# Row maxima of windowed scores: four heads' blocks of 32 queries against one head's blocks of 128

## The chip, the cores and the metric

The kernel runs on one core of a Trainium2 chip. The metric is the device time of one execution in microseconds (us), the median of several runs. The core has five engines that run side by side, each with its own queue of instructions in fixed order: TensorE (PE in the profile; PEld is its weight load), VectorE (DVE), ScalarE (ACT), GpSimd (POOL) and SyncE (SP), which here only issues DMAs. Matmul results go to PSUM, from which VectorE and ScalarE read.

## What is computed

Two independent parts stand side by side in the output. Part A is attention with 32 heads of 18 dimensions over 2048 positions, in a sliding window of 256 keys; part B is a state-space convolution over 2048 positions in 576 channels, done as a product in the frequency domain.

```python
H = 32; Dh = D // H; W = 256                 # S = 2048, D = 576
scores = jnp.einsum("bhqd,bhkd->bhqk", q, k) * (Dh ** -0.5)
mask = (idx[:, None] - idx[None, :] >= 0) & (idx[:, None] - idx[None, :] < W)
scores = jnp.where(mask[None, None], scores, -1e9)
p = _softmax(scores, axis=-1)
o = jnp.einsum("bhqk,bhkd->bhqd", p, v)
...
return jnp.concatenate([a, b], axis=-1)
```

The softmax needs the largest score of each query among its 256 keys (or something near it). The change is in how that maximum is found.

## The kernel before

Up to about 475 us the kernel projects x to q, k and v (in split halves of 16 bits), builds the convolution's tables and transforms u and the convolution's taps. The attention follows, with the convolution's frequency products and inverse transform woven in.

The attention has 16 units, `i` from 0 to 15: `hf, g = divmod(i, 8)`, half of the positions (1024 queries) and a group of four heads. A unit's tensor `Q` is 128 x 2 x 1024: heads lie in two row halves `u` (rows 0 to 53 and 64 to 117, three parts of 18 dimensions in each) and two column planes `b`. `K` has the same layout with 1280 columns, 256 of them ahead of the unit's first query. Row 54 of each half of `Q` holds the row maximum, row 54 of `K` a large negative constant, so that the score matmuls of `scores` (L738) subtract the maximum by themselves. Three sets of `Q` and `K` rotate.

`gmax(i)` computes the maxima of unit `i`. It begins by copying `Q` into `qb`, block-diagonally (L688): for each 32 queries of a plane, 64 columns, the first 32 with the upper half's head and the last 32 with the lower half's. Then it goes over 32 blocks `t` of 32 queries. For each block one PSUM tile of the pool `ring` (three buffers of 128 x 512) takes two matmuls, one for each plane, of up to 288 keys (L697), so that its 128 rows are four heads by 32 queries. VectorE adds a bias that masks the triangles at both ends and takes the maximum over the 288 in one instruction, whose sum register is then read out (L704). After every two blocks the generator yields. At the end the 128 x 32 maxima are scaled, transposed in 32 x 32 blocks (L711, L712), and four DMAs on SP's queue, due with the next item, write them into row 54 of `Q` (L715; in the profile they appear under L133, which issues what is due).

`attention` (L835) writes out the order by hand. It goes over 96 items, six for each unit (two halves `c` of 512 queries, three banks of score blocks) and merges in each item several generators in proportion: `scores` of item n (TensorE, then the exponentials on ScalarE, L740, then masks on GpSimd, L749), `gmax` of the unit after next, `values` of item n-2 (L761), and a share of `conv`. `gmax(i + 2)` starts in item 3 of unit i and ends by item 3 of unit i+1, with 17 yields over six items; `gmax(0)` runs before the items, merged with the rest of the taps' transform `s1k` (L520), and `gmax(1)` in the first three items. `load_unit(i + 2)` (L676, L677) issues the loads of a unit in item 0 of unit i. The normalisation `norm` of a finished unit (L797 on, with L812, L820 and L823 on VectorE) advances one step per item.

`conv` shares `ring` with `gmax`: two matmul tiles of the signal (L561) that ScalarE copies out (L588), two of the taps (L561 again) that VectorE multiplies with them from PSUM (L591 to L594), sums on GpSimd (L598, L599), and two tiles of the inverse transform (L569) that ScalarE copies out (L571). The output projection (L967) uses `ring` too. A tile of `ring` is handed out in the order of the program, and a matmul into it waits until the tile three places earlier has been read.

Of the kernel before, what the change touches and what calls it, by code (L numbers as in the profile page):

```python
# [11 lines left out]
F32 = mybir.dt.float32  # L12
F16 = mybir.dt.float16
BF = mybir.dt.bfloat16
I32 = mybir.dt.int32
AF = mybir.ActivationFunctionType
OP = mybir.AluOpType
AX = mybir.AxisListType
# [21 lines left out]
def constants():  # L40
    c = {}
    tau = 2 * np.pi
    l1, l2, f1, f2 = np.arange(32), np.arange(64), np.arange(32), np.arange(64)
    ph = -tau * np.outer(l1, f1 + 0.25) / 32
    w1 = np.zeros((128, 2, 128))
    for s in range(4):
        w1[s * 32:s * 32 + 32, 0, s::4] = np.cos(ph)
        w1[s * 32:s * 32 + 32, 1, s::4] = np.sin(ph)
    w2 = np.zeros((128, 32, 128))
    i1 = np.zeros((128, 32, 128))  # L50
    for f in range(32):
        ph = -tau * np.outer(l2, f + 0.25 + 32 * f2) / 2048
        co, si = np.cos(ph), np.sin(ph)
        w2[0:64, f, 0:64], w2[64:128, f, 0:64] = co, -si
        w2[0:64, f, 64:128], w2[64:128, f, 64:128] = si, co
        i1[0:64, f, 0:64], i1[64:128, f, 0:64] = co.T, si.T
        i1[0:64, f, 64:128], i1[64:128, f, 64:128] = -si.T, co.T
    ph = tau * np.outer(f1 + 0.25, l1) / 32
    i2 = np.zeros((128, 64))
    for p in range(2):  # L60
        i2[p * 64:p * 64 + 32, p * 32:p * 32 + 32] = np.cos(ph) / 2048
        i2[p * 64 + 32:p * 64 + 64, p * 32:p * 32 + 32] = -np.sin(ph) / 2048
    mult = {"c_cm": np.arange(64), "c_ct": np.arange(32) + 0.5, "c_ca": np.r_[64 * np.arange(8), 512 * np.arange(4)],
            "c_cp": np.r_[np.zeros(8), np.full(4, 31.5)]}
    for nm, v in mult.items():
        t = np.zeros((3, GC, GC, len(v)))
        for g in range(GC):
            t[:, g, g] = v
        c[nm] = t.reshape(96, GC, len(v))
    bias = np.zeros((128, 2, 32))  # L70
    for p in range(128):
        bias[p, 0, :p % 32 + 1] = -1e30
        bias[p, 1, p % 32 + 1:] = -1e30
    c["c_w1"], c["c_w2"], c["c_i1"], c["c_i2"] = w1, w2, i1, i2
    c["c_id"], c["c_bias"] = np.eye(128), bias
    return {k: np.ascontiguousarray(v.astype(ml_dtypes.bfloat16 if k in mult else np.float32)) for k, v in c.items()}
# [40 lines left out]
class Kernel:  # L117
# [527 lines left out]
    def att_setup(self):  # L645
        nc, a, ap = self.nc, self.a, self.p["att"]
        self.ident = ap.tile([128, 128], F32, name="ident")
        nc.sync.dma_start(self.ident, a["c_id"])
        self.bias = ap.tile([128, 288], F32, name="bias")
        nc.vector.memset(self.bias, 0.0)  # L650
        for e in range(2):
            nc.sync.dma_start(self.bias[:, 256 * e:256 * e + 32], a["c_bias"][:, e])
        self.qb = ap.tile([128, 2, 32, 64], F16, name="qb")
        nc.gpsimd.memset(self.qb, 0.0)
        self.sets = []
        for b in range(3):
            d = {"Q": ap.tile([128, 2, HQ], F16, name="Q%d" % b), "K": ap.tile([128, 2, HK], F16, name="K%d" % b)}
            nc.vector.memset(d["Q"], 0.0)
            for h in (32, 96):
                nc.vector.memset(d["K"][h:h + 32].bitcast(I32), 0xF800F800 - (1 << 32))  # L660
            self.sets.append(d)
        self.od = self.p["dram"].tile([2, D, L], F16, name="od")
# [19 lines left out]

    def gmax(self, i):

        nc, (hf, g), d = self.nc, divmod(i, 8), self.sets[i % 3]
        m = self.p["m"].tile([128, 32], F32, name="m")
        for u in range(2):
            nc.vector.tensor_copy(self.qb[64 * u:64 * u + 54, :, :, 32 * u:32 * u + 32],  # L688
                                  d["Q"][64 * u:64 * u + 54].rearrange("p b (t q) -> p b t q", q=32))
        yield  # L690
        pair = []
        for t in range(32):
            ps = self.p["ring"].tile([128, 512], F32, name="r")
            k0 = 32 * t if hf > 0 or t >= 8 else 256
            n = 32 * t + 288 - k0
            for b in range(2):
                nc.tensor.matmul(ps[64 * b:64 * b + 64, :n], self.qb[:, b, t, :], d["K"][:, b, k0:k0 + n],  # L697
                                 start=True, stop=True, skip_group_check=True)
            pair.append((t, n, ps))
            if t % 2 == 0:  # L700
                continue
            for t, n, ps in pair:
                jk = self.p["m"].tile([128, 288], F32, name="jk")
                nc.vector.tensor_tensor_reduce(out=jk[:, :n], in0=ps[:, :n], in1=self.bias[:, 288 - n:], scale=1.0,  # L704
                                               scalar=-3e38, op0=OP.add, op1=OP.max, accum_out=m[:, t:t + 1])
            pair = []
            yield
        yield
        m16 = self.p["m"].tile([128, 32], F16, name="m16")
        mt = self.p["m"].tile([128, 32], F16, name="mt")  # L710
        nc.vector.tensor_scalar(m16, m, 2.0 ** -15, None, op0=OP.mult)  # L711
        nc.vector.transpose(mt, m16)  # L712
        for j in range(4):
            r = 64 * (j % 2) + 54
            self.after(1, nc.sync.dma_start, d["Q"][r:r + 1, j // 2].rearrange("o (s q) -> o s q", q=32),  # L715
                       mt[32 * j:32 * j + 32])
        yield

    BL = [(0, 0, 0, 1), (128, 2, 0, 3), (512, 1, 0, 2), (768, 4, 2, 4), (1024, 3, 1, 4), (1408, 5, 3, 4)]
# [379 lines left out]
```

## Time and profile before

| what | us |
|---|---|
| three runs | 1017.26, 1021.78, 1023.51 (median 1021.78) |
| the profiled execution | 1019.01 |
| its span in the profile | 1017.3 |
| mean granted TensorE clock in it | 0.972 of full |

The profile shows one execution. For each engine it gives the time in which it worked and, before each instruction, the idle time and what ended it. The chain of waits follows the work back from the last instruction to what released each step. A matmul of two or four pieces is recorded as several matmuls, and a few per cent of the records are missing. Busy times include the overlap of neighbours on one engine only once.

### The profile page before, as it was taken

The page shows a single profiled execution, that of the slowest core. Times are in us where ns is not written, and L with a number is a line of the kernel's source. Part 1 is how long each engine was busy: PE and PEld are TensorE (multiplying, and loading weights), DVE is VectorE, ACT ScalarE, POOL GpSimd, SP SyncE. Part 2 cuts the span into 40 slices and gives each one's busy share as a digit, 9 for nine tenths or more (in the row PEclk, how much of TensorE's full clock was granted, in tenths as well). Part 3 has the DMA queues.
Part 4 walks back from the last instruction along what each step waited for, and adds up shares of the span by engine and source line. Part 5 has one row for each costly group of instructions (what it writes and reads, how often), then busy time and mean ns, then how long its engine had stood idle before and what let it go on. Part 6 is the DMA issues. An engine that isn't in the chain of part 4 may idle for free.

```text
span 1017.3 us, 26963 instructions
## 1 busy us (share of the span) xinstructions
PE 836.2 (82%) x10364; PEld 447.1 (44%) x10364; DVE 691.9 (68%) x1821; ACT 561.8 (55%) x901; POOL 590.6 (58%) x727
## 2 busy tenths in 40 slices
PE   0287979888899999788888888778888999988687
PEld 0034645464566557454433333323333444444245
DVE  5689487567574566557677778767777766668454
ACT  1456656557666765235555555555555655634470
POOL 2119557475686677101657675748676757676680
PEclk9999989999999999799999999989999999999899
DMA  8824535424443542746465675645555584578863
GB/s 299 254 69 122 141 91 131 98 74 121 123 105 76 133 100 74 226 169 199 122 152 126 177 172 144 164 119 150 136 136 152 132 189 114 157 199 231 229 181 126
DMA packets 139240, 150.35 MB, mean 148 GB/s; under 512 B 37464, under 2 KB 106248, under 8 KB 138344
## 3 DMA queue, kind: packets, MB, share of 16 engines
q1 hardware_dynamic: 131144, 131.75, 48.3%
q0 software_dynamic: 6512, 15.04, 5.6%
q10 hardware_dynamic: 1456, 1.84, 0.6%
q8 instruction: 82, 1.34, 0.6%
q14 instruction: 46, 0.38, 0.1%
HBM read 86.30 MB, written 61.01 MB: 145 GB/s over the span
## 4 chain that ended last, share of the span: by engine, by line
PE 27%; DVE 11%; DMA 6%; issue 6%; ACT 3%; SPq 2%; POOL 2%; DVEq 0%; ACTq 0%; POOLq 0%
PE r L697 5%; PE po L761 5%; PE r L967 5%; PE r L561 3%; PE r L569 3%; PE ST L738 3%; DVE jk L704 2%; PE pp L520 2%; DVE qb L688 2%; ACT P L740 1%; DVE osb L820 1%; DMA out_dram<-t 1%; DVE t L591 1%; DMA raw<-in_wo_dram 1%; DMA tx<-gx 1%
## 5 line engine op out<-in xcount | busy, mean ns | idle before, releaser
L704 DVE CUSTOM_DVE_ANT_0 jk<-r,bias 128x288 f32<-128x288 f32 (+7 forms) x512 | 200.1, 434 | 90.4 <-PE r L697 88.3
L749 POOL TENSOR_SCALAR_AFFINE_SELECT P<-P 128x512 f32<-128x512 f32 x240 | 167.8, 728 | 149.3 <-ACT P L740 146.6
L740 ACT ACTIVATE P<-ST,esc 128x1024 f32<-128x1024 f32 (+1 forms) x192 | 202.7, 1060 | 91.8 <-PE ST L738 91.2
L441 POOL TENSOR_TENSOR m<-A,tr 128x1024 f32<-128x1024 f32 x72 | 144.3, 2026 | 84.1 <-PE kp L479 84.0
L697 PE MATMUL r<-K,qb 128*64 128x288 f16 (+7 forms) x1024 | 129.1, 295 | 45.2 <-DVE qb L688 12.0
L697 PEld LDWEIGHTS <-qb 128*64 128x64 f16 x1024 | 59.8, 109 | 128.4 <-issue 69.4
L761 PE MATMUL po<-P,V 128*32 128x256 f32 (+2 forms) x1408 | 99.9, 397 | 16.3 <-ACT osb L769 7.0
L598 POOL TENSOR_TENSOR Y<-t,t 64x288 f32<-64x288 f32 x64 | 55.0, 859 | 77.9 <-DVE t L593 76.0
L479 PE MATMUL kp<-Q,m 128*32 128x64 f32 x4608 | 80.3, 221 | 10.9 <-issue 2.8
L479 PEld LDWEIGHTS kp<-Q,m 128*32 128x32 f32 x4608 | 69.3, 110 | 41.7 <-issue 22.4
L738 PE MATMUL ST<-Q,K 64*128 64x384 f16 (+2 forms) x704 | 72.7, 280 | 0.0
L382 DVE TENSOR_TENSOR k<-x,k 128x512 f32<-128x512 f32 (+1 forms) x54 | 34.1, 642 | 36.7 <-ACT k L381 36.3
L144 ACT ACTIVATE g<-pp 128x288 f32<-128x288 f32 x96 | 37.9, 414 | 37.4 <-PE pp L520 29.9
L761 PEld LDWEIGHTS po<-P,V 128*32 128x32 f32 x1408 | 36.3, 110 | 50.3 <-issue 34.2
L419 POOL TENSOR_TENSOR tr<-tr,mab 128x768 f32<-128x768 f32 x18 | 33.4, 1858 | 42.5 <-ACT tr L388 42.5
L179 PE MATMUL pp<-xh,wh 128*128 128x512 f16 x180 | 48.4, 387 | 9.4 <-ACT xh L210 8.9
L599 POOL TENSOR_TENSOR Y<-t,t 64x288 f32<-64x288 f32 x64 | 53.3, 832 | 3.7
L179 PEld LDWEIGHTS <-wh 128*128 128x128 f16 x324 | 31.5, 99 | 51.2 <-issue 17.8
L383 DVE TENSOR_SCALAR ab<-k 128x512 int32<-128x512 int32 (+1 forms) x54 | 50.5, 947 | 0.4
L561 PE MATMUL r<-tx,w 128*64 128x288 f32 x256 | 42.4, 441 | 9.0 <-ACT X L588 4.8
L520 PE MATMUL pp<-ut,w 128*128 128x288 f32 x128 | 40.4, 437 | 10.0 <-DVE qst L341 6.9
L821 ACT ACTIVATE oh<-osb 128x512 f16<-128x512 f32 x26 | 16.4, 632 | 55.9 <-DVE osb L820 55.3
(169 smaller groups left out, 1729.1 us busy)
## 6 DMA issues: line engine op xcount, KB each, us to landing
qd<-qst SPq DMA_DIRECT2D x72, 128.0 KB
gx<-g SPq DMA_DIRECT2D x32, 288.0 KB
gk<-g SPq DMA_DIRECT2D x32, 288.0 KB
tx<-gx SPq DMA_DIRECT2D x32, 288.0 KB
tk<-gk SPq DMA_DIRECT2D x32, 288.0 KB
h<-ho SPq DMA_DIRECT2D x16, 576.0 KB
Q<-qd SPq DMA_DIRECT2D x32, 216.0 KB
raw<-in_x_dram SPq DMA_DIRECT2D x16, 320.0 KB
```

The lines of the kernel that those rows point to most:

```text
L179: self.nc.tensor.matmul(ps, u, v, start=(i == 0), stop=(i == len(ops) - 1))
L441: self.nc.gpsimd.tensor_tensor(m, A[:, ch, a0:a0 + 8].unsqueeze(3).to_broadcast(sh), tr[:, ch, part, 0:8].unsqueeze(2).to_broadcast(sh), o ...
L479: nc.tensor.matmul(kp[32 * st:32 * st + 32, c % 2 * JJ2 + j, :], m[:, ch, a0:a0 + 32], Q[:, ch, term % 2, :], start=(term == 0), stop=(ter ...
L520: nc.tensor.matmul(ps, self.w1[:, part, :], src[:, o:o + k], start=True, stop=True)
L561: nc.tensor.matmul(ps[64 * par:64 * par + 64], w2[:, par, 64 * part:64 * part + 64], t[:, par, 2 * hs:2 * hs + 2, :], start=True, stop=True)
L598: nc.gpsimd.tensor_tensor(Y[par][0:64], t1[sl, 0], t2[sl, 0], op=OP.subtract)
L697: nc.tensor.matmul(ps[64 * b:64 * b + 64, :n], self.qb[:, b, t, :], d["K"][:, b, k0:k0 + n], start=True, stop=True, skip_group_check=True)
L704: nc.vector.tensor_tensor_reduce(out=jk[:, :n], in0=ps[:, :n], in1=self.bias[:, 288 - n:], scale=1.0, scalar=-3e38, op0=OP.add, op1=OP.max ...
L738: nc.tensor.matmul(ps[:, u, o:o + n], d["K"][h, jp, k0:k0 + 128], d["Q"][h, jp, q0:q0 + n], start=True, stop=True, skip_group_check=True)
L740: nc.scalar.activation(pt[:, 2 * jp:2 * jp + 2, lo:hi], ps[:, :, lo:hi], AF.Exp, scale=self.esc)
L749: nc.gpsimd.affine_select(v, v, pattern=[[0, 4], [sg, 128]], compare_op=OP.is_ge, fill=0.0, base=-1 if far else 0, channel_multiplier=-sg)
L761: nc.tensor.matmul(self.po[32 * j:32 * j + 32, t0 * 128:t1 * 128], V[:, kb * 76 + 19 * j:kb * 76 + 19 * j + 32], pt[:, j, o:o + (t1 - t0) ...
```

## The change

The maxima are computed one head at a time, for 128 queries in a tile. `qb`, its memset and its copies are gone; the matmuls take 128 columns of `Q` (54 rows of one half) as weights and up to 384 keys of the same half of `K`, and a step makes two PSUM tiles, one for each row half. There are again 16 steps and yields per unit, with two tiles each. In a full tile the first 128 columns are the far keys and the last 128 the near ones; query p may see far key j if j > p and near key j if j <= p. So the two triangles fit together: where the mask constant is not zero (near keys that are not allowed), a predicated copy writes the far key's score over the near one's in PSUM, and one maximum over columns 128 to 383 follows. Tiles at the very beginning of the sequence, with 128 or 256 keys, are done as before with a bias of the new shape. The maxima come out in another arrangement, so eight DMAs of 16 pieces each write them into `Q`, instead of four of 32.

```diff
-    bias = np.zeros((128, 2, 32))
+    bias = np.zeros((128, 256))
     for p in range(128):
-        bias[p, 0, :p % 32 + 1] = -1e30
-        bias[p, 1, p % 32 + 1:] = -1e30
+        bias[p, 129 + p:] = -1e30
...
-        self.bias = ap.tile([128, 288], F32, name="bias")
-        nc.vector.memset(self.bias, 0.0)
-        for e in range(2):
-            nc.sync.dma_start(self.bias[:, 256 * e:256 * e + 32], a["c_bias"][:, e])
-        self.qb = ap.tile([128, 2, 32, 64], F16, name="qb")
-        nc.gpsimd.memset(self.qb, 0.0)
+        self.bias = ap.tile([128, 256], F32, name="bias")
+        nc.sync.dma_start(self.bias, a["c_bias"])
...
-        m = self.p["m"].tile([128, 32], F32, name="m")
-        for u in range(2):
-            nc.vector.tensor_copy(self.qb[64 * u:64 * u + 54, :, :, 32 * u:32 * u + 32],
-                                  d["Q"][64 * u:64 * u + 54].rearrange("p b (t q) -> p b t q", q=32))
-        yield
-        pair = []
-        for t in range(32):
-            ps = self.p["ring"].tile([128, 512], F32, name="r")
-            k0 = 32 * t if hf > 0 or t >= 8 else 256
-            n = 32 * t + 288 - k0
-            for b in range(2):
-                nc.tensor.matmul(ps[64 * b:64 * b + 64, :n], self.qb[:, b, t, :], d["K"][:, b, k0:k0 + n],
-                                 start=True, stop=True, skip_group_check=True)
-            pair.append((t, n, ps))
-            if t % 2 == 0:
-                continue
-            for t, n, ps in pair:
-                jk = self.p["m"].tile([128, 288], F32, name="jk")
-                nc.vector.tensor_tensor_reduce(out=jk[:, :n], in0=ps[:, :n], in1=self.bias[:, 288 - n:], scale=1.0,
-                                               scalar=-3e38, op0=OP.add, op1=OP.max, accum_out=m[:, t:t + 1])
+        m = self.p["m"].tile([128, 2, 16], F32, name="m")
+        yield
+        for n in range(16):
+            t, b = n // 2, n % 2
+            k0 = 128 * t if hf > 0 or t >= 2 else 256
+            w = 128 * t + 384 - k0
             pair = []
+            for u in range(2):
+                ps = self.p["ring"].tile([128, 512], F32, name="r")
+                h = slice(64 * u, 64 * u + 54)
+                nc.tensor.matmul(ps[:, :w], d["Q"][h, b, 128 * t:128 * t + 128], d["K"][h, b, k0:k0 + w],
+                                 start=True, stop=True)
+                pair.append(ps)
+            for u, ps in enumerate(pair):
+                mx = m[:, u, 8 * b + t:8 * b + t + 1]
+                if w == 384:
+                    nc.vector.copy_predicated(ps[:, 256:384], self.bias[:, 128:256].bitcast(I32), ps[:, 0:128])
+                    nc.vector.tensor_reduce(mx, ps[:, 128:384], axis=AX.X, op=OP.max)
+                else:
+                    jk = self.p["m"].tile([128, 256], F32, name="jk")
+                    nc.vector.tensor_tensor_reduce(out=jk[:, :w], in0=ps[:, :w], in1=self.bias[:, 256 - w:], scale=1.0,
+                                                   scalar=-3e38, op0=OP.add, op1=OP.max, accum_out=mx)
             yield
...
-            r = 64 * (j % 2) + 54
-            self.after(1, nc.sync.dma_start, d["Q"][r:r + 1, j // 2].rearrange("o (s q) -> o s q", q=32),
-                       mt[32 * j:32 * j + 32])
+            for u in range(2):
+                self.after(1, nc.sync.dma_start,
+                           d["Q"][64 * u + 54:64 * u + 55].rearrange("o b (t q) -> o (b t) q", q=128)[:, :, 32 * j:32 * j + 32],
+                           mt[32 * j + 16 * u:32 * j + 16 * u + 16])
```

More of the change, by code (lines that the diff above doesn't have):

```diff
@@ L710, in gmax @@
         mt = self.p["m"].tile([128, 32], F16, name="mt")
-        nc.vector.tensor_scalar(m16, m, 2.0 ** -15, None, op0=OP.mult)
+        nc.vector.tensor_scalar(m16, m.rearrange("p u n -> p (u n)"), 2.0 ** -15, None, op0=OP.mult)
         nc.vector.transpose(mt, m16)
         for j in range(4):
-            r = 64 * (j % 2) + 54
-            self.after(1, nc.sync.dma_start, d["Q"][r:r + 1, j // 2].rearrange("o (s q) -> o s q", q=32),
-                       mt[32 * j:32 * j + 32])
+            for u in range(2):
+                self.after(1, nc.sync.dma_start,
+                           d["Q"][64 * u + 54:64 * u + 55].rearrange("o b (t q) -> o (b t) q", q=128)[:, :, 32 * j:32 * j + 32],
+                           mt[32 * j + 16 * u:32 * j + 16 * u + 16])
         yield
```

## The prediction

> **What bounds the kernel now.** The page first: span, busy times and the chain of work that ended last.
>
> ```profile
> span 1017.3 us, 26963 instructions
> PE 836.2 (82%) x10364; PEld 447.1 (44%) x10364; DVE 691.9 (68%) x1821; ACT 561.8 (55%) x901; POOL 590.6 (58%) x727
> PE r L697 5%; PE po L761 5%; PE r L967 5%; PE r L561 3%; PE r L569 3%; PE ST L738 3%; DVE jk L704 2%; PE pp L520 2%; DVE qb L688 2%; ACT P L740 1%; DVE osb L820 1%; DMA out_dram<-t 1%; DVE t L591 1%; DMA raw<-in_wo_dram 1%; DMA tx<-gx 1%
> ```
>
> No engine fills the span, and the chain passes from engine to engine. So I cut the span where maxima are computed. The windows view gives all engines first (PE, PEld, DVE, ACT, POOL, clock, DMA), then the instructions of L704 (the maxima), L688 (copies into qb) and L697 (their matmuls) alone:
>
> ```profile
> 440.00:476.00 36.00, 30.98 (x182) 18.44 (x180) 22.30 (x105) 16.64 (x33) 1.88 (x3) 0.95 0.61 198
> 476.00:900.00 424.00, 358.58 (x3376) 163.75 (x3377) 316.42 (x1124) 241.99 (x350) 281.61 (x404) 0.99 0.58 147
> ...
> 476.00:900.00 424.00, 167.32 (x840) 0.99 0.58 147
> ...
> 476.00:900.00 424.00, 25.02 (x26) 0.99 0.58 147
> ...
> 476.00:900.00 424.00, 107.05 (x842) 48.76 (x843) 0.99 0.58 147
> ```
>
> From 476 to 900 us VectorE is busy 75% and TensorE 85%, and the maxima are more than half of VectorE's work. The waits of that stretch, and its chain by line:
>
> ```profile
> DVE jk L704 <- PE r L697: 82.0, 82, 3.5
> ...
> by line: issue 11.5%; PE r L697 10.6%; PE po L761 9.7%; PE r L561 7.9%; PE r L569 6.9%; PE ST L738 5.8%; DVE jk L704 4.5%; PE r L967 4.1%; DVE qb L688 3.6%; ACT P L740 3.0%; DVE osb L820 3.0%; DVE t L591 2.7%; DMA raw<-in_wo_dram 2.7%; DMA
> ```
>
> VectorE idles 108 us there, 82 of them before a maximum whose matmul is late, in 82 places. L704 ran 840/2 = 420 recorded maxima, some 210 pairs; so in about 60% of the pairs the scores lay ready and VectorE was the late one. Both engines wait for each other through the three PSUM buffers of the ring: a matmul needs the buffer that VectorE (or ScalarE) read three tiles earlier, and TensorE's queue is in order, so scores and values behind it wait too.
>
> **The change part by part.** The costs per instruction, from the groups with shapes kept apart (busy us, mean ns):
>
> ```profile
> L704 DVE CUSTOM_DVE_ANT_0 jk<-r,bias 128x288 f32<-128x288 f32 x448 | 183.3, 452 | 79.7 <-PE r L697 77.9
> L697 PE MATMUL r<-K,qb 128*64 128x288 f16 x896 | 117.2, 302 | 33.4 <-DVE t L592 9.1 <-ACT X L588 4.8 <-DVE m L704 4.7
> L738 PE MATMUL ST<-Q,K 64*128 64x384 f16 x256 | 43.0, 333 | 0.0
> L688 DVE COPY qb<-Q 54x2048 f16<-54x2048 f16 x32 | 29.7, 927 | 0.5
> L704 DVE CUSTOM_DVE_ANT_0 jk<-r,bias 128x256 f32<-128x256 f32 x8 | 3.4, 420 | 0.0
> L704 DVE CUSTOM_DVE_ANT_0 jk<-r,bias 128x128 f32<-128x128 f32 x8 | 2.3, 287 | 0.0
> L943 DVE TENSOR_REDUCE go<-r 128x1 f32<-128x128 f32 x1 | 0.3, 278 | 0.0
> ```
>
> and from the timeline (start, length), how close instructions follow each other:
>
> ```profile
> 501.00 0.45 DVE L591 TENSOR_TENSOR t<-X,r 128x288 f32<-128x288 f32 x1 [1.02 <-PE r L561]
> 501.37 0.45 DVE L592 TENSOR_TENSOR t<-X,r 128x288 f32<-128x288 f32 x1
> ...
> 502.46 0.45 DVE L704 CUSTOM_DVE_ANT_0 jk<-r,bias 128x288 f32<-128x288 f32 x1
> 502.84 0.09 DVE L704 DVE_READ_ACCUMULATOR2_ANT m<- 128x1 f32 x1
> 502.84 0.45 DVE L704 CUSTOM_DVE_ANT_0 jk<-r,bias 128x288 f32<-128x288 f32 x1
> ...
> 516.68 0.35 DVE L808 RECIPROCAL den<-den 128x32 f32<-128x32 f32 x1
> 517.06 0.21 DVE L810 STREAM_TRANSPOSE dent<-den 128x32 f32<-128x32 f32 x1
> ```
>
> *The maxima.* An instruction of 0.45 us that depends on nothing new lets the next one start 0.08 us before its end (501.00 to 501.37); one that reads its predecessor's result starts 0.03 us after its end (516.68 + 0.35 to 517.06). A maximum over 288 thus holds VectorE for 0.38 us (502.46 to 502.84). After, a full tile is a predicated copy of 128 and a maximum over 256 that waits for it. The trace has no predicated copy and no write of VectorE to PSUM. Nearest are 0.287 us (128 wide, PSUM and SBUF in) below and 0.42 us (256 wide, as if each element took two steps) above; I take 0.285, as 128 elements with two inputs is what it is. The lower bound is 0.19 us, the same operation cut by the 0.08 us of overlap; the whole wait cannot vanish, since the reduction reads the copy's output. The reduction over 256: the one reduction from PSUM took 278 ns over 128, and 288 against 128 wide (452 and 287 ns) make 1.03 ns per element, so 0.41 us, of which 0.08 overlap: 0.33. Together 0.285 + 0.03 + 0.33 = 0.645 us against 0.38: +0.265 on each of 448 full tiles, +119 us. Bounds: 0.55 and 0.78 per tile, +76 and +179 us. Behind the new wait stand, on VectorE, the pair's second tile and the conv's products; for both, and for the ring's buffer, TensorE waits.
>
> [...]
>
> *Short tiles* of the first half's units: 64 before and after, of 32 to 256 elements before, of 128 or 256 after; +3 us.
>
> *qb.* 32 copies of 0.93 us go: -29.7 us of VectorE. On the chain they are 3.6% of 424 us, 15 us. What is late next is the conv's kernel half on TensorE, then its four products on VectorE.
>
> *Matmuls.* Four of 288 columns per pair become two of 384 in two row halves, the form of L738. By busy time: 117.2/896 x 4 = 0.52 us before, 43.0/256 x 2 = 0.34 after: -0.18 us a pair, about -40 us of TensorE over 224 full pairs; weight loads halve.
>
> *DMAs.* The maxima go back in eight issues instead of four on SP's queue, with the same elements.
>
> ```profile
> 541.03 2.44 SPq L133 DMA_DIRECT2D Q<-mt  x4
> ...
> 555.20 0.31 SPq L676 DMA_DIRECT2D Q<-qd  x1
> ```
>
> Four take 2.44 us; four more, between nothing (half-size) and +2.44 us. Behind them stand the conv's loads for its next step; who needs the maxima is the next unit's first score matmul, in the item that also issues the load at 555.20, 14 us later. That covers it: nothing. Without that cover it would cost up to 2.4 us in each of 14 units. The gone memset of qb (once, on POOL before the attention) and the constant in one DMA: nothing.
>
> *How much of it shows.* Net VectorE work is +119 + 3 - 30 = +92 us, and the idle it can fill is of that size, so the walk along a unit decides. I walked 700 to 732 us, a unit with full tiles, with 0.645 us a tile, a buffer free 0.73 us after its copy starts, and 0.1 us less per pair of matmuls:
>
> ```profile
> 705.23 1.19 PE L561 MATMUL r<-tk,w 128*64 128x288 f32 x8
> ...
> 705.30 1.59 DVE L688 COPY qb<-Q 54x2048 f16<-54x2048 f16 x2
> 706.92 0.45 DVE L591 TENSOR_TENSOR t<-X,r 128x288 f32<-128x288 f32 x1
> ...
> 711.67 0.46 DVE L704 CUSTOM_DVE_ANT_0 jk<-r,bias 128x288 f32<-128x288 f32 x1 [1.69 <-PE r L697]
> ...
> 719.61 0.45 DVE L704 CUSTOM_DVE_ANT_0 jk<-r,bias 128x288 f32<-128x288 f32 x1
> ...
> 720.37 1.24 DVE L820 TENSOR_TENSOR osb<-osb,spread 128x512 f32<-128x512 f32 x1
> ...
> 721.52 0.45 DVE L704 CUSTOM_DVE_ANT_0 jk<-r,bias 128x288 f32<-128x288 f32 x1
> ...
> 722.03 0.30 PEld L569 LDWEIGHTS r<-Y,i 128*128 128x128 f32 x2 [0.37 <-DVE m L704]
> ...
> 727.43 0.20 PEld L561 LDWEIGHTS r<-tx,w 128*64 128x64 f32 x4 [0.96 <-DVE m L704]
> ...
> 732.21 0.68 PEld L561 LDWEIGHTS r<-tk,w 128*64 128x64 f32 x8 [0.62 <-DVE m L704]
> ```
>
> Up to 705.3 the six tiles cost little, as VectorE waited for TensorE between the pairs (about +0.4). Then qb's 1.59 us go and the products start when their input is there: its first half leaves TensorE about 0.6 us after 705.23, so at 705.8 instead of 706.92, 1.1 us earlier; so at 710 the schedule is some 0.8 us ahead, in spite of four longer tiles. Four tiles from 711.67 use that up: +0.2 at 713. In the second half there is no qb, and VectorE has the norm's multiplications between the tiles: two longer tiles from 719.61 push the 1.24 us at 720.37 and the tile at 721.52 back, whose buffer the inverse's second matmul awaits; 722.03 becomes about 722.9 (+0.85). The next such wait, 727.43, comes 1.45 later, and at 732 it is about 2.0 us. So a unit loses 2.0 us of its added 32 x 0.265 - 1.9 = 6.6. Eight units (8 to 15) have 32 full tiles: +16. Units 1 to 7 have 24, and their short ones stand where the chain goes over GpSimd's masks: 1.4 each, +10. Unit 0 lies beside the kernel transform's last matmuls before 476; VectorE is 62% busy there (22.30 of 36), and only a group's fourth tile waits for a buffer, about 0.2 us longer in each of some ten steps, +2. The chain of the first place and TensorE's timeline of the second:
>
> ```profile
> 515.70 1.82 POOL P L749 x3
> 517.55 1.07 PE po L761 x16
> ```
>
> ```profile
> 442.27 0.31 PE L697 MATMUL r<-K,qb 128*64 128x288 f16 x2 [0.43 <-DVE m L704]
> ```
>
> Sum: 1019.0 us (profiled execution: span 1017.3 and 1.7 around it) + 16 + 10 + 2 = 1047. That execution lies 2.8 under the median of the three runs, 1021.8; on the median it is **1050 us**, my forecast.
>
> **The rivals.** (1) *TensorE's relief wins*: the longer maxima fall into VectorE's 108 us of idle, while the chain loses qb (15 us) and a third of L697's 45 us (10.6% of 424), 0.18/0.52 x 45 = 16. That gives 1022 - 31 = **991 us**. For it: TensorE is the busier engine and leads the chain. Against it: 60% of pairs find VectorE late already. It decides if the walk's exposure, 26 of 92 us, is nought. (2) *The gains and losses cancel*: the same relief on a chain that keeps about half of the loss, **1020 us**; for it speaks the first half of the walked unit, which came out at +0.2. (3) *The predicated copy is dear*: at two steps per element, 0.42 us, a tile takes 0.78, and VectorE's load from 476 to 900 becomes 316 - 25 + 364 x 0.40 = 437 us in a stretch of 424 (364: the 420 recorded less 7 x 8 short ones). Then it bounds, and nearly two thirds of the extra 448 x 0.135 = 60 us shows: +38, **1087 us**. The write to PSUM, which no row shows, speaks for it. That the edit does something else than it says I give nothing: in the order of instructions ScalarE's and GpSimd's lists keep their sequence, and TensorE's and VectorE's change at these lines alone.
>
> **How the numbers follow.** Forecast (1034 to 1066) 0.50; rival 1, 0.16; rival 2, 0.16; rival 3, 0.18. The range holds the forecast, rivals 2 and 3 and a part of rival 1's slope: 1008 to 1092; the likeliest case's own is 1034 to 1066. A change of under 1% (1012 to 1032) can't be told from none here. Slower: 0.50 + 0.18 = 0.68; same 0.16; faster 0.16.
>
> **What would show it.** In the profile after: copies of about 0.29 us and reductions of about 0.41, started 0.32 apart; VectorE's busy time up by some 90 us, near 87% or more in the attention stretch; TensorE's L697 matmuls down to some 75 us; waits of VectorE for r shorter, waits of TensorE for VectorE's reductions longer; ScalarE and GpSimd unchanged. Copies of 0.2 or 0.4 us, a chain still led by TensorE with VectorE's idle unfilled, or the eight DMAs showing before a score matmul would make it wrong.

## The result, and the profile after

| | median us (runs) | ratio to the kernel before, 95% interval |
|---|---|---|
| before, on the same chip | 1019.52 (4) | |
| changed | 1089.72 (4) | 1.0697 (1.0634 to 1.0761) |

The kernel is slower by 70 us. The forecast was slower by 28, at 1050; the measured time lies inside the stated range, at the price given for the third rival, but that rival's mechanism is not what happened. The page of the changed kernel; its line numbers lie one lower than before in most of the code (L760 is the old L761, L560 the old L561, L568 the old L569), L693 holds the maxima's matmuls, L699 the predicated copy, L700 the reduction:

```profile
span 1088.8 us, 25761 instructions
...
PE 885.0 (81%) x9852; PEld 437.1 (40%) x9852; DVE 767.9 (71%) x1788; ACT 562.9 (52%) x901; POOL 567.7 (52%) x726
...
L693 PE MATMUL r<-K,Q 54*128 54x384 f16 (+2 forms) x512 | 149.8, 347 | 64.2 <-DVE m L700 38.0
L700 DVE TENSOR_REDUCE m<-r 128x1 f32<-128x256 f32 x448 | 190.3, 425 | 15.5
...
L699 DVE COPY_PREDICATED r<-bias,r 128x128 f32<-128x128 int32 x448 | 128.5, 287 | 73.9 <-PE r L693 73.9
```

The copy takes 0.287 us and the reduction 0.425: almost the prices that the prediction took (0.285 and 0.41). Their spacing, from VectorE's timeline (start, length):

```profile
542.18 0.29 DVE L699 COPY_PREDICATED r<-bias,r 128x128 f32<-128x128 int32 x1
542.50 0.42 DVE L700 TENSOR_REDUCE m<-r 128x1 f32<-128x256 f32 x1
542.85 0.29 DVE L699 COPY_PREDICATED r<-bias,r 128x128 f32<-128x128 int32 x1
543.17 0.42 DVE L700 TENSOR_REDUCE m<-r 128x1 f32<-128x256 f32 x1
```

From copy to copy 0.67 us (0.66 to 0.67 in longer rows), where the prediction had 0.645. So the work on VectorE was priced right: 448 x 0.285 = 128 us more in the full tiles. But the stretch from 476 to 900 us, by engine as before, and its chain by line say what it did to the others:

```profile
476.00:900.00 424.00, 354.21 (x2527) 134.25 (x2528) 333.94 (x984) 213.35 (x309) 230.01 (x346) 0.87 0.52 130
```

```profile
by line: PE po L760 13.5%; DVE m L700 13.4%; PE r L560 12.9%; PE r L568 9.5%; DVE r L699 8.3%; PE r L693 7.9%; issue 6.6%; DVE t L590 2.5%; PE r L966 2.3%; DVE t L592 2.0%; DVE t L591 2.0%; PE ST L737 1.9%; DVE t L593 1.8%; DVE osb L819 1.6
```

VectorE is busy 79% (333.94 of 424), not the 87% or more that was forecast, and over the whole span its busy time rose by 76 us (691.9 to 767.9), where some 90 were forecast. Copy and reduction hold 21.7% of the chain from 480 to 900 us, where maxima and qb held 8.1% before. TensorE's lines still lead that chain, with 48% against 32 for VectorE's in the line above; what grew is VectorE's share. TensorE is about as busy as before (84 against 85%) with half as many matmuls for the maxima: one takes longer (359 ns for 384 columns, 302 for 288 before), they overlap less (448 x 0.359 / 136.6 = 1.2 of them at a time on average, 896 x 0.302 / 117.2 = 2.3 before), so that those of the full tiles keep it busy for 136.6 us instead of 117.2, and its granted clock fell from 0.99 to 0.87.

The places where the time was lost can be read from the transposes of the maxima (L712 before, L710 after), one per unit, in VectorE's timeline:

| from transpose to transpose | before | after | difference | forecast |
|---|---|---|---|---|
| to unit 0's | 461.33 | 464.33 | +3.0 | +2 |
| unit 1 | 19.87 | 28.57 | +8.7 | +1.4 |
| units 2 to 7 | 192.78 | 212.63 | +19.9 | +8.4 |
| units 8 to 15 | 271.76 | 310.41 | +38.6 | +16 |
| from unit 15's to the end | 73.3 | 74.7 | +1.4 | 0 |

The sum is 71.6, the distance of the two profiled executions (1019.01 and 1090.60). Unit 1 shows the mechanism most plainly, as its 16 steps are crowded into three items instead of six. TensorE's timeline in it:

```profile
478.76 0.50 PE L693 MATMUL r<-K,Q 54*128 54x384 f16 x1 [0.17 <-DVE m L700]
479.42 0.50 PE L693 MATMUL r<-K,Q 54*128 54x384 f16 x1 [0.17 <-DVE m L700]
480.08 0.50 PE L693 MATMUL r<-K,Q 54*128 54x384 f16 x1 [0.17 <-DVE m L700]
480.75 0.50 PE L693 MATMUL r<-K,Q 54*128 54x384 f16 x1 [0.17 <-DVE m L700]
...
489.40 0.33 PE L693 MATMUL r<-K,Q 54*128 54x384 f16 x1 [0.33 <-DVE m L700]
490.06 0.33 PE L693 MATMUL r<-K,Q 54*128 54x384 f16 x1 [0.33 <-DVE m L700]
```

One matmul every 0.66 us, each released by a reduction: TensorE goes at VectorE's pace, tile by tile, through the ring of three buffers, and whatever stands behind these matmuls in its queue waits with them. The last two take 0.33 us instead of 0.50, at a granted clock of 0.99 (489.40 to 490.70) instead of 0.50 (478.76 to 484.00), and they still start 0.66 us apart. The two matmuls of a pair no longer run side by side in these rows, as each waits for a buffer of its own.

Not all of unit 1's 8.7 us is that. Its first score matmuls need unit 0's maxima, which eight DMAs now write instead of four. SyncE's queue and TensorE's first score matmul, before:

```profile
461.68 2.50 SPq L133 DMA_DIRECT2D Q<-mt  x4
...
464.52 0.34 PE L738 MATMUL ST<-Q,K 64*128 64x384 f16 x2
```

and after:

```profile
464.69 5.03 SPq L132 DMA_DIRECT2D Q<-mt  x8
...
470.94 0.48 PE L737 MATMUL ST<-Q,K 64*128 64x384 f16 x1 [0.16 <-DMA Q<-mt]
```

The first of these score matmuls (470.30) starts 6.0 us behind unit 0's transpose, where it was 3.2 before. With four DMAs (e8 below) unit 1 takes 25.2 us instead of 28.6. The granted clock in unit 1 is low as well, 0.66 against 0.91 before (0.74 in e8).

In units 12 and 13 the clock is full before and after. The windows of the two units, before and then after (the clock is the third figure from the end):

```profile
800.40:837.82 37.42, 34.69 (x334) 17.40 (x328) 24.70 (x87) 21.10 (x31) 22.68 (x32) 1.00 0.75 170
837.82:872.26 34.44, 32.18 (x312) 16.48 (x312) 23.27 (x83) 20.03 (x31) 21.73 (x31) 1.00 0.35 101
```

```profile
853.46:895.15 41.69, 35.42 (x296) 16.26 (x292) 30.39 (x85) 20.64 (x31) 21.02 (x33) 1.00 0.66 154
895.15:933.94 38.79, 33.43 (x284) 15.76 (x281) 28.98 (x82) 20.55 (x30) 20.95 (x33) 1.00 0.31 91
```

They lose 4.3 and 4.4 us, near the mean of units 8 to 15, 4.8, without any loss of clock.

### The profile page after: what moved, and what is told of

It reads as the page before. It is cut to its first block, busy times and chain, and to the rows that moved or that the text cites. A ratio compares the mean times of both kernels' runs of the same rounds, so it can differ in the third digit from the quotient of the medians.

```text
span 1088.8 us, 25761 instructions
## 1 busy us (share of the span) xinstructions
PE 885.0 (81%) x9852; PEld 437.1 (40%) x9852; DVE 767.9 (71%) x1788; ACT 562.9 (52%) x901; POOL 567.7 (52%) x726
## 4 chain that ended last, share of the span: by engine, by line
PE 46%; DVE 27%; issue 8%; DMA 8%; ACT 5%; SPq 3%; POOL 2%; ACTq 0%; DVEq 0%; POOLq 0%
PE pp L178 8%; DVE m L700 8%; PE po L760 7%; PE r L560 5%; PE r L966 5%; DVE r L699 5%; PE pp L519 4%; PE r L693 4%; PE r L568 4%; PE kp L478 4%; PE x L370 2%; DMA c_ct<-in_c_ct_dram 2%; SPq L132 1%; PE ST L737 1%; DVE xh L211 1%
## 5 line engine op out<-in xcount | busy, mean ns | idle before, releaser
L748 POOL TENSOR_SCALAR_AFFINE_SELECT P<-P 128x512 f32<-128x512 f32 x240 | 155.4, 676 | 210.4 <-ACT P L739 207.7
L693 PE MATMUL r<-K,Q 54*128 54x384 f16 (+2 forms) x512 | 149.8, 347 | 64.2 <-DVE m L700 38.0
L700 DVE TENSOR_REDUCE m<-r 128x1 f32<-128x256 f32 x448 | 190.3, 425 | 15.5
L699 DVE COPY_PREDICATED r<-bias,r 128x128 f32<-128x128 int32 x448 | 128.5, 287 | 73.9 <-PE r L693 73.9
L760 PE MATMUL po<-P,V 128*32 128x256 f32 (+2 forms) x1408 | 112.0, 437 | 8.4 <-POOL P L748 4.1
L693 PEld LDWEIGHTS <-Q 54*128 54x128 f16 x512 | 40.8, 95 | 177.4 <-DVE m L700 113.7
L597 POOL TENSOR_TENSOR Y<-t,t 64x288 f32<-64x288 f32 x64 | 52.0, 812 | 109.9 <-DVE t L592 107.9
L737 PE MATMUL ST<-Q,K 64*128 64x384 f16 (+2 forms) x704 | 94.7, 295 | 2.9 <-issue 2.7
L760 PEld LDWEIGHTS po<-P,V 128*32 128x32 f32 x1408 | 37.6, 116 | 51.8 <-issue 33.8
L568 PE MATMUL r<-Y,i 128*128 128x288 f32 x128 | 52.8, 524 | 6.3 <-ACT ho L570 3.0
L560 PE MATMUL r<-tx,w 128*64 128x288 f32 x256 | 48.1, 481 | 9.1 <-DVE m L700 5.7
L560 PE MATMUL r<-tk,w 128*64 128x288 f32 x256 | 47.5, 477 | 8.3 <-DVE m L700 6.8
```

The lines of the kernel that those rows point to most:

```text
L560: nc.tensor.matmul(ps[64 * par:64 * par + 64], w2[:, par, 64 * part:64 * part + 64], t[:, par, 2 * hs:2 * hs + 2, :], start=True, stop=True)
L568: nc.tensor.matmul(pair[par], i1[:, par, :], Y[par], start=True, stop=True)
L693: nc.tensor.matmul(ps[:, :w], d["Q"][h, b, 128 * t:128 * t + 128], d["K"][h, b, k0:k0 + w], start=True, stop=True)
L699: nc.vector.copy_predicated(ps[:, 256:384], self.bias[:, 128:256].bitcast(I32), ps[:, 0:128])
L700: nc.vector.tensor_reduce(mx, ps[:, 128:384], axis=AX.X, op=OP.max)
L737: nc.tensor.matmul(ps[:, u, o:o + n], d["K"][h, jp, k0:k0 + 128], d["Q"][h, jp, q0:q0 + n], start=True, stop=True, skip_group_check=True)
```

## The experiments

Two theories at the start. **W**: the time is lost where TensorE and VectorE wait for each other's buffers, so it follows VectorE's work per tile; the lower clock only follows. **C**: the thinner matmuls (54 rows of the array instead of 128) and the waits let the clock fall, and that is about half of the loss. Ratios below are to the kernel before on the same chip; one per cent is 10.2 us.

**e1_old_matmuls** keeps the old tiles, matmuls and qb, and gives VectorE alone the new load; the copy's mask is zero, so it changes nothing, and the maximum leaves out the mask at the ends.

```diff
             for t, n, ps in pair:
+                if n == 288:
+                    nc.vector.copy_predicated(ps[:, 0:112], self.bias[:, 64:176].bitcast(I32), ps[:, 128:240])
+                    nc.vector.tensor_reduce(m[:, t:t + 1], ps[:, :n], axis=AX.X, op=OP.max)
+                    continue
```

> The kernel before, with blocks of 32 queries, qb and its matmuls; only VectorE's work per full tile is made that of the change: a predicated copy of 112 columns whose mask is zero, then one maximum over the 288 columns without the masks at the ends, about 0.66 us a tile instead of 0.38. Theory W (the time is lost where TensorE and VectorE wait for each other's ring buffers; the lower clock only follows): the whole loss comes back, and qb with it, 1090 to 1110 us. Theory C (the thinner matmuls of the change let the granted clock fall, and that is about half of the loss): the clock stays near 0.97 and the time is 1045 to 1070 us.

1098.7 us, 1.0792 (1.0742 to 1.0842), clock 0.939. Its VectorE timeline:

```profile
575.08 0.27 DVE L704 COPY_PREDICATED r<-bias,r 128x112 f32<-128x112 int32 x1
575.39 0.46 DVE L705 TENSOR_REDUCE m<-r 128x1 f32<-128x288 f32 x1
575.76 0.27 DVE L704 COPY_PREDICATED r<-bias,r 128x112 f32<-128x112 int32 x1
```

0.68 us a tile, 0.30 more than before, 134 us in 448 tiles; 81 us of them show, 60%. So the whole loss is there without one new matmul: W. The clock fell here too, with matmuls that were not thinner, so that this run alone does not separate the waits from a clock that falls with them.

**e2_no_copy** is the changed kernel without its predicated copy; far keys and mask are left out.

```diff
-                    nc.vector.copy_predicated(ps[:, 256:384], self.bias[:, 128:256].bitcast(I32), ps[:, 0:128])
                     nc.vector.tensor_reduce(mx, ps[:, 128:384], axis=AX.X, op=OP.max)
```

> The changed kernel without the predicated copy: each full tile has one maximum over its last 256 columns, so the far keys and the mask are left out; about 0.35 us a tile. W: VectorE is quicker than in the kernel before and qb is gone, 985 to 1005 us at a clock near 0.97. C: the matmuls alone lower the clock to 0.95 or less, and the time is 1005 to 1030 us.

1013.0 us, 0.9937 (0.9904 to 0.9969), clock 0.957. The copy and the wait for it are worth 7.6% together, more than the whole change. But both theories had something else: the time is above W's range, at C's lower part, and the clock between them. New matmuls and the missing qb bring almost nothing here.

**e3_one_maximum** takes one maximum over all 384 columns of a full tile, without copy and mask.

```diff
-                    nc.vector.copy_predicated(ps[:, 256:384], self.bias[:, 128:256].bitcast(I32), ps[:, 0:128])
-                    nc.vector.tensor_reduce(mx, ps[:, 128:384], axis=AX.X, op=OP.max)
+                    nc.vector.tensor_reduce(mx, ps[:, 0:384], axis=AX.X, op=OP.max)
```

> The changed kernel with one maximum over all 384 columns of a full tile and no predicated copy and no mask: the value taken off is a maximum over more keys than the window. About 0.48 us a tile. W: 1000 to 1025 us. C: clock 0.93 to 0.95, 1020 to 1050 us.

1037.7 us, 1.0173 (1.0114 to 1.0232), clock 0.934: above W's range, inside C's. From e2 on, VectorE's work per tile rises by 0.13 us and the time by 2.4%, which is 42% of the 58 us added; from here to the changed kernel it is 61% of 87 us.

**e4_matmuls_twice** issues each of the maxima's matmuls twice, into the same place.

```diff
-                nc.tensor.matmul(ps[:, :w], d["Q"][h, b, 128 * t:128 * t + 128], d["K"][h, b, k0:k0 + w],
-                                 start=True, stop=True)
+                for _ in range(2):
+                    nc.tensor.matmul(ps[:, :w], d["Q"][h, b, 128 * t:128 * t + 128], d["K"][h, b, k0:k0 + w],
+                                     start=True, stop=True)
```

> The changed kernel with each of its maxima's matmuls issued twice into the same place, VectorE's work unchanged: more activity on TensorE, and a tile that is ready some 0.16 to 0.3 us later. W: slower still, 1095 to 1115 us, whatever the clock. C: the clock rises to 0.95 or more and the time falls to 1060 to 1085 us.

1089.3 us, 1.0705 (1.0652 to 1.0757), clock 0.956. The clock rose as C said and the time did not move: C's time missed, and W's, which had it slower, missed too. In units 8 to 15 the clock is 0.98 here, nearly the 0.99 of before, and they take 312.8 us, against 310.4 in the changed kernel and 271.8 before (one profiled execution each).

**e5_fillers** lets TensorE work behind a pair's first matmul, in columns that nobody reads.

```diff
+                if w == 384 and u == 0:
+                    for _ in range(4):
+                        nc.tensor.matmul(ps[:, 384:512], d["Q"][h, b, 128 * t:128 * t + 128], d["K"][h, b, k0:k0 + 128],
+                                         start=True, stop=True, skip_group_check=True)
```

> The changed kernel with four more matmuls of 128 columns behind each full pair's first one, into the columns 384 to 511 of its tile, which nobody reads: TensorE works where it would wait for the second tile's buffer, and no maximum waits for them by its data. W: the time stays at 1085 to 1100 us whatever the clock does. C (the clock costs half of the loss): the clock is 0.95 or more and the time 1050 to 1070 us.

1099.2 us, 1.0810 (1.0778 to 1.0842), clock 0.932: inside W's range, and not faster; but the clock rose little, so C was hardly put to the test.

**e6_qb_kept** puts the two copies into qb back into the changed kernel, where nobody reads them.

```diff
+        for u in range(2):
+            nc.vector.tensor_copy(self.qb[64 * u:64 * u + 54, :, :, 32 * u:32 * u + 32],
+                                  d["Q"][64 * u:64 * u + 54].rearrange("p b (t q) -> p b t q", q=32))
```

> The changed kernel, in which the two copies into qb per unit stay in place although nobody reads them: 30 us of VectorE are put back. If the copies are worth what their share of the chain said, 15 us: 1100 to 1108 us. If VectorE takes them in idle time: within 4 us of the changed kernel, 1086 to 1094. If all of them show: 1115 to 1122.

1101.9 us, 1.0855 (1.0795 to 1.0915): 1.6% above the changed kernel, 16 us. The missing qb is worth what its share of the chain said.

**e7_plain_maximum** is the kernel before with a plain maximum over a full tile's 288 columns, without the mask.

```diff
+                if n == 288:
+                    nc.vector.tensor_reduce(m[:, t:t + 1], ps[:, :n], axis=AX.X, op=OP.max)
+                    continue
```

> The kernel before with a plain maximum over the 288 columns of a full tile instead of bias and maximum, so the mask at both ends is left out: about 0.36 us a tile, near the 0.345 of the changed kernel without its copy (1013 us), but with the old matmuls and with qb. If the new matmuls and the missing qb are worth the 25 us that the prediction gave them: 1005 to 1018 us here, no, then this kernel would stand 20 to 30 us above 1013, at 1030 to 1045. If they are worth little beside equal work on VectorE: 1005 to 1018.

1014.9 us, 0.9977 (0.9956 to 0.9997), clock 0.972. Beside e2 it has old matmuls, qb, and 0.015 us more a tile, and is 0.4% slower, 4 us, of which half of 448 x 0.015, 3 us, is the tile. It lies in the range for matmuls and qb that are worth little. If qb is worth the 16 us of e6 here too, the new matmuls with their DMAs cost some 15 us; if it is worth the 5 of e11 below, some 4. e1 and e6 point the same way with long tiles: with qb in both, the new matmuls stand 0.6% above the old ones, 6 us, although their tile is 0.015 us shorter; but that is no larger than the intervals. What these runs show is that the new matmuls save nothing.

**e8_four_dmas** writes the maxima back with four DMAs over two rows of Q each.

```diff
-            for u in range(2):
-                self.after(1, nc.sync.dma_start,
-                           d["Q"][64 * u + 54:64 * u + 55].rearrange("o b (t q) -> o (b t) q", q=128)[:, :, 32 * j:32 * j + 32],
-                           mt[32 * j + 16 * u:32 * j + 16 * u + 16])
+            self.after(1, nc.sync.dma_start,
+                       d["Q"][54:119:64].rearrange("o b (t q) -> o (b t) q", q=128)[:, :, 32 * j:32 * j + 32],
+                       mt[32 * j:32 * j + 32])
```

> The changed kernel with the maxima written back by four DMAs of 32 pieces instead of eight of 16. The prediction gave the four extra issues nothing: 1086 to 1094 us. If SyncE's queue, which takes 6.6 us for eight in the trace of the changed kernel, delays what stands behind them: 1065 to 1082.

1086.6 us, 1.0690 (1.0652 to 1.0729): the same as the changed kernel. SyncE's queue in the changed kernel, and in this one:

```profile
632.02 6.59 SPq L132 DMA_DIRECT2D Q<-mt  x8
```

```profile
635.35 2.60 SPq L132 DMA_DIRECT2D Q<-mt  x4
```

The eight took 6.59 us, 4 more, where the prediction allowed at most 2.4; over the whole kernel that does not show, though unit 1 alone is 3.3 us shorter with four.

**e9_no_copy_twice** doubles the matmuls of e2 (with e2's parts left out), where there is little clock to regain.

```diff
-                nc.tensor.matmul(ps[:, :w], d["Q"][h, b, 128 * t:128 * t + 128], d["K"][h, b, k0:k0 + w],
-                                 start=True, stop=True)
+                for _ in range(2):
+                    nc.tensor.matmul(ps[:, :w], d["Q"][h, b, 128 * t:128 * t + 128], d["K"][h, b, k0:k0 + w],
+                                     start=True, stop=True)
...
-                    nc.vector.copy_predicated(ps[:, 256:384], self.bias[:, 128:256].bitcast(I32), ps[:, 0:128])
```

> The changed kernel without the predicated copy (far keys and mask left out, 1013 us at a clock of 0.957) and with each of the maxima's matmuls issued twice. In the changed kernel itself the doubling cost nothing while the clock rose from 0.921 to 0.956. If the clock did not matter there (W), the doubled matmuls cost nothing here either: 1008 to 1018 us. If the regained clock paid for them there (C), they cost what they are worth here, where little clock is to be regained: 1025 to 1040 us.

1017.5 us, 0.9993 (0.9960 to 1.0027), clock 0.964: inside W's range, and 0.6% above e2, 6 us. In the changed kernel the same doubling cost 0.1%. The difference, 5 us, is what the regained clock may have paid there, and it is no larger than the intervals.

**e10_copies_first** puts both copies of a pair ahead of both reductions.

```diff
+            if w == 384:
+                for ps in pair:
+                    nc.vector.copy_predicated(ps[:, 256:384], self.bias[:, 128:256].bitcast(I32), ps[:, 0:128])
             for u, ps in enumerate(pair):
...
-                    nc.vector.copy_predicated(ps[:, 256:384], self.bias[:, 128:256].bitcast(I32), ps[:, 0:128])
                     nc.vector.tensor_reduce(mx, ps[:, 128:384], axis=AX.X, op=OP.max)
```

> The changed kernel with both copies of a pair ahead of both maxima, so that no maximum waits for the copy right in front of it: about 0.20 + 0.34 us a tile instead of 0.665, some 55 us less on VectorE. W, with 0.6 of VectorE's work showing as in the kernel with the old matmuls: 1050 to 1062 us. If the loss is the clock's or TensorE's: 1075 to 1092.

1067.9 us, 1.0488 (1.0416 to 1.0561), clock 0.929: 2.1% below the changed kernel, 21 us, which lies between W's range and the other one. Its timeline:

```profile
540.80 0.48 DVE L698 COPY_PREDICATED r<-bias,r 128x128 f32<-128x128 int32 x2
541.19 0.75 DVE L702 TENSOR_REDUCE m<-r 128x1 f32<-128x256 f32 x2
541.86 1.65 DVE L824 TENSOR_TENSOR oh<-osb,oh 128x512 f16<-128x512 f32 x1
```

A pair takes 1.06 us, 0.53 a tile: 0.135 less, 60 us in all, and 35% of it shows. The first buffer of a pair is now released later than its own work would need, behind the second one's copy, which gives some of it back; that reason is argued, not shown.

**e11_before_no_qb** is the kernel before without qb: four matmuls per block, one for each head, into its 32 rows.

```diff
             for b in range(2):
-                nc.tensor.matmul(ps[64 * b:64 * b + 64, :n], self.qb[:, b, t, :], d["K"][:, b, k0:k0 + n],
-                                 start=True, stop=True, skip_group_check=True)
+                for u in range(2):
+                    h, r = slice(64 * u, 64 * u + 54), 64 * b + 32 * u
+                    nc.tensor.matmul(ps[r:r + 32, :n], d["Q"][h, b, 32 * t:32 * t + 32], d["K"][h, b, k0:k0 + n],
+                                     start=True, stop=True, skip_group_check=True)
```

> The kernel before, with bias and maximum over 288 as they were, but without qb: each block of 32 queries takes four matmuls, one for each head, straight from Q into its 32 rows of the tile. If the copies into qb are worth 12 us, as they were in the changed kernel, and four narrow matmuls cost no more than two: 1003 to 1012 us. If the doubled number of matmuls costs as much: 1013 to 1025.

1013.4 us, 0.9948 (0.9918 to 0.9979), clock 0.964: half a per cent faster than the kernel before and 7% faster than the changed one, with the same maxima as before. Its matmuls in the groups:

```profile
L694 PE MATMUL r<-K,Q 54*32 54x288 f16 x1792 | 117.2, 299 | 24.5 <-DVE t L592 5.5 <-DVE t L639 4.6 <-DVE m L701 4.4
```

Twice as many matmuls take the same busy time as the 896 before, 117.2 us: at 299 ns each, more than four of them run side by side on average (1792 x 0.299 / 117.2 = 4.6). Leaving qb out brought 16 us in the changed kernel and some 5 here, at the lower end of the range for matmuls that cost as much; how far the doubled matmuls take from it is not separated.

**e12_full_fillers** repeats e5 with fillers over all rows of the array.

```diff
+                if w == 384 and u == 0:
+                    for _ in range(3):
+                        nc.tensor.matmul(ps[:, 384:512], d["K"][:, b, k0:k0 + 128], d["K"][:, b, k0:k0 + 128],
+                                         start=True, stop=True, skip_group_check=True)
```

> The changed kernel with three more matmuls of 128 columns over all 128 rows of the array behind each full pair's first one, into columns of its tile that nobody reads; the four fillers over half the rows raised the clock only from 0.921 to 0.932 and cost 9.5 us. If the clock follows how much of the array works, it comes to 0.95 or more here. C: then the time falls to 1055 to 1078 us. W: it stays at 1088 to 1105 us.

1100.8 us, 1.0844 (1.0795 to 1.0892), clock 0.957. The stretch from 476 to 900 us in it:

```profile
476.00:900.00 424.00, 376.15 (x3028) 154.26 (x3026) 331.55 (x983) 211.94 (x309) 232.56 (x348) 0.95 0.52 130
```

The clock is back at 0.95 there, TensorE has 22 us more work in the stretch than in the changed kernel, and the time is not better. e5 and e12 keep TensorE busy equally long over the span (922.2 and 921.0 us), at 0.932 and 0.957, and stand at 1.0810 and 1.0844: the higher clock brought no time that shows. W.

W's ranges held in e1, e5, e9 and e12 and missed in e2, e3, e4 and e10, by 6 to 13 us; C's held in e2 and e3 and missed in e1, e4, e5, e9 and e12, by 23 to 29 us in e1, e5 and e12. W is the better account, and its sizes are rough.

## Why the prediction was wrong

The direction and the price of the operations were right, and in the main the mechanism too: VectorE's longer tile holds the ring's buffers, and TensorE waits for them. The step that failed is **"How much of it shows"**. The prediction had VectorE's net work at +92 us and let 28 of it show: 2.0 us in each of units 8 to 15, 1.4 in each of units 1 to 7, and 2 in unit 0. Measured by the spacing of its tiles, the net work is 128 + 3 - 30 = +101 us, and 70 us show: 4.8 in each of units 8 to 15, 3.3 in each of units 2 to 7, 8.7 in unit 1 and 3 in unit 0. (By busy time it is 76 us, as a full tile held VectorE for 183.3/448 = 0.41 us on average before, not the 0.38 of close neighbours; by that count nearly all shows.)

- *The price of a tile* was 0.645 us, measured 0.665; 9 us of VectorE's work. (The copy's lower bound of 0.19 us should be 0.21 by the working's own subtraction, 0.287 less 0.08.) The taken value in each choice (one step per element, 0.03 us behind a result) was right, so rival 3 fell, although its time of 1087 us is close to the measured one.
- *The walk.* The stretch that it was made on, counted from the transpose at 705.16, has its counterpart in the changed kernel from 745.44 on. The matmul at 732.21 then started 27.05 us behind the transpose, and now, at 774.46, 29.02 behind it: +1.97, where the walk gave 2.0, 0.4 of them from before the transpose. That agreement is in part luck, as the way there is another. Counted from the transposes, the inverse's second matmul (722.03 before, 762.05 now) came 0.3 us earlier, where the walk had it some 0.45 later; then VectorE's next two multiplications took 2.52 us instead of 1.81; and 0.86 of the 1.97 us is a slower clock, which the walk did not have (next point). What failed besides is that one unit, walked up to 732, stood for all. The whole unit lost 3.3 (32.6 to 35.9 us), the mean of units 8 to 15 is 4.8, units 2 to 7 lost 3.3 each, not 1.4, and unit 1 lost 8.7: some 3.3 by the eight DMAs (e8), most of the rest, 5.5 us from e2 to the changed kernel, where its tiles follow each other without other work between them.
- *The clock in the walk* was full. In this unit's end it was not:

```profile
772.60 1.93 PE L760 MATMUL po<-P,V 128*32 128x128 f32 x16
774.46 2.19 PE L560 MATMUL r<-tk,w 128*64 128x288 f32 x8
```

 The granted clock was 0.50 there (772.60 to 776.60). The same groups took 1.07 and 1.19 us before (731.21 and 732.21), at 1.00 (731.21 to 733.40). That is 1.9 us on the path in one unit. It would be a cause on its own, were it not for e4 and e12, in which the clock was raised to 0.956 and 0.957 by added matmuls and the time stayed or rose, and for units 12 and 13, which lost 4.3 and 4.4 us at full clock. The added matmuls have a price of their own (6 us in e9), so a few us for the clock are not excluded; half of the loss is, unless they cost far more in the changed kernel than in e9.
- *qb* was priced at 15 us from its share of the chain; e6 measured 16. In e11, on the old tiles and with twice the matmuls, leaving it out brought 5.
- *The matmuls* were to save 0.1 us per pair in the walk, and 16 us in the first rival. They saved nothing that shows: by e7 against e2 they stand 4 to 15 us worse than the old ones, by e6 against e1 some 6 to 10, neither of them sure. In the profile a pair's two matmuls wait for two buffers and start one by one, and L693's busy time is 149.8 us where about 75 were forecast. What makes up such a loss, if there is one, stays open.
- *The DMAs* took 6.59 us of SyncE's queue instead of up to 4.9, and cost nothing that shows over the whole kernel (e8), as forecast. But at the start of unit 1 they do show before a score matmul, which the prediction named as a sign of being wrong: its cover of 14 us, read in a later unit, is not there.
- *The first rival* (TensorE's relief wins) and the second one had relief from the matmuls where there was none; only qb's came. VectorE's idle was not free room: e1 fills it with 134 us and 81 come out as time.

The sum as it stands now: 128 x 0.6 = +77 for the full tiles with e1's share, -16 for qb, and about +10 for the matmuls: +71, against 70 measured. It is made after the fact from differences between the same runs, so that it closes is no check.

## What to carry to other kernels

TensorE and VectorE, each in its own order, handed buffers to and fro through a ring of three here, and VectorE, busy 75% of the time, had little idle to give: of work added to each hand-over, 35 to 61% showed in the pairs of runs, and with e1's load VectorE came to 82% (346.92 us from 476 to 900). A walk along the trace prices one place at best; it must be made on the crowded places too, and its result compared with the gross sum times a cautious share before the smaller number is taken. Merging the work into fewer, larger matmuls brought nothing that shows here, not even in e2, where VectorE reads each tile only once.

## What the runs showed of the hardware

TensorE's granted clock was half in places where TensorE was busy all the time. In the changed kernel, in windows of 2 us:

```profile
720.00:722.00 2.00, 2.00 (x7) 0.44 (x6) 0.71 (x3) 0.82 (x2) 1.81 (x4) 0.50 0.60 217
722.00:724.00 2.00, 1.79 (x17) 0.70 (x17) 1.93 (x6) 0.21 (x1) 2.00 (x3) 0.50 0.72 199
...
744.00:746.00 2.00, 2.00 (x21) 0.69 (x19) 1.86 (x8) 1.11 (x1) 2.00 (x4) 1.00 1.15 233
```

Of the 22 windows from 716 to 760 us six show 0.50, ten 1.00 and six a value between. In windows of 0.25 us over the same stretch 66 of 176 show 0.50, 104 show 1.00 and six a value between, so the values between in the longer windows come nearly all from these two in turn. What sets the clock is not shown. It did not go with busy time alone: from 476 to 900 us TensorE was busy 358.58 us at 0.99 before and 354.21 us at 0.87 in the changed kernel. Doubled matmuls over 54 of 128 rows brought the mean from 0.921 to 0.956 (e4), three short ones over 128 rows brought 0.957 (e12), and four of the same length over 54 rows only 0.932 (e5).

The predicated copy from PSUM to PSUM took 0.287 us for 128 columns, as long as the bias and maximum of that width before (L704, 128x128, 287 ns).
